# Layer 2 of a fused attention and two-layer MoE kernel in two halves of three slabs over all blocks

## The chip, the core and the metric

The kernel runs on one core of one Trainium2 chip. The metric is the device time of one execution, in microseconds (us). Several executions are timed, and their median is given. A profiled execution gives the trace; its span, from the first to the last instruction, is a little shorter than its own time. Engines: PE is TensorE (matrix products; PEld are its weight loads), DVE is VectorE, ACT is ScalarE, POOL is GpSimd, SP is SyncE, whose queue issues all DMAs here. L12 is line 12 of the kernel.

## The reference

```python
# attention: q, k, v of 4 x 8 heads x 576 positions x 64, a causal window of 64
scores = scale * q @ k.T, outside the window -1e9; softmax; @ v
x = attention, heads joined: 2304 tokens x 512
# layer 1, d_ff 1536
xn = x / sqrt(mean(x * x) + 1e-6) * rms_g
x = (silu(xn @ w_gate) * (xn @ w_val)) @ w_out
# layer 2, d_ff 1536
out = (sigmoid(x @ w_gate2) * (x @ w_val2)) @ w_out2
```

## The kernel before

The 2304 tokens are six blocks of 384. Attention makes a block's 512 x 384 input (st_s, st_tr, st_pv; L387 to L480), beside which its squares are summed and scaled (rms_first: L525 makes diagonal matrices of the scale, the product L526 applies it, L529 takes the result over). Values enter TensorE as pairs of fp16 numbers, high and low, and each product is three matmuls (high x high, high x low, low x high). The split of a block's input is split_first: ScalarE writes the high half (L534), VectorE subtracts it (L535).

Layer 1 treats blocks 0 and 1 plainly: gate and value products (moe_g, moe_v, L574 in mm3, with L587 and L597 on VectorE behind them), the gate's multiplication (moe_h, L608), the output product (moe_o, L623 to L625). The pairs of blocks 2, 3 and 4, 5 of layer 1 and all three pairs of layer 2 use seven products for a 2 x 2 scheme of sub-blocks instead of eight: moe_w(l, p, s) does slab s (256 of d_ff) of pair p, with the products in L784, copies L797 on ScalarE, additions L787 on VectorE and a split into fp16 pairs at the end. The operand of such a product is one of seven *forms* of a pair's input, made by xform_items (split L711, L712) and kept in one set of seven buffers (xform). In layer 2 the forms of pairs 1 and 2 are stored to DRAM (L715) and fetched when the pair's turn comes (fetch_form, L700).

The output products of layer 2 are moe_p(p, ss, c), for the slabs ss and half c of the rows: 7 forms x slabs x 3 matmuls (L888), with PSUM results going to SBUF through a ScalarE copy (L896, the first group of slabs), a scaled addition on VectorE (L898, later groups) or a plain copy (L891). With the last group `give` stores the result (L904).

Weights are 36 packages of 1 MB, 18 a layer (0 to 11: gate and value of six slabs; 12 to 17: output). w_load (L233) fetches one; w_max takes its largest element on VectorE (L243), over the partitions on POOL (L246), and makes scales of it with a few tiny operations (L247 to L254). w_conv and w_split turn it into fp16 pairs (L270 and L335 on ScalarE, L271, L272 and L337 on VectorE); layer 2's packages have sums made for the seven products too (w_sums).

Before the change the weights of layer 2 share one scale over all six slabs (w_l2_scale). It needs every package's maximum, so all 18 are loaded once during layer 1, for w_max alone, and once more for conversion (`again`). The packages' loads and their conversions are hung behind steps of the main sequence (LATER). PLAN2 says for each pair which slabs and which output groups follow:

```python
PLAN2 = [(0, 1, (0, 1), 2, 3, (2, 3), 4, 5, (4, 5)), (0, 1, (0, 1), 2, 3, (2, 3), 4, 5, (4, 5)), (0, 1, 2, (0, 1), 3, 4, (2, 3), 5, (4, 5))]
```

Buffers for intermediate results come from a list of free pieces of the weight areas (`room`, `take`, `early`). The final order of each engine's instructions is fixed by a compressed table (ORDER, applied by arrange after the program is built).

Of the kernel before, what the change touches and what calls it, by code (L numbers as in the profile page):

```python
# [48 lines left out]
AGAIN = (0, 1, 2, 3, 12, 13, 4, 5, 14, 6, 7, 15, 8, 9, 16, 10, 11, 17)  # L49
RAW2 = {j: (2, (56, 64)[i % 2]) for i, j in enumerate(AGAIN)}  # L50
# [61 lines left out]
def fused_kernel(ctx, tc, q, k, v, w_gate, w_val, w_out, rms_g, w2_gate, w2_val, w2_out, const16, const32, out, plan, asked):  # L112
# [47 lines left out]
    ocm = cst.tile([P, 1], F32, name="ocm")  # L160
# [136 lines left out]
    def w_l2_scale():  # L297
        pgv = pw[:, 1, 0:12].rearrange("p (s m) -> p s m", m=2)
        pf = small("pf", NG)
        V.tensor_tensor(out=pf, in0=pgv[:, :, 1], in1=pw[:, 1, 12:18], op=ALU.mult)  # L300
        cm = small("cm")
        V.tensor_reduce(out=cm, in_=pf, axis=AX.X, op=ALU.max)
        ic = small("ic")
        V.reciprocal(out=ic, in_=cm)
        V.tensor_scalar(out=hs2, in0=pf, scalar1=ic, scalar2=2.0 ** -23, op0=ALU.mult, op1=ALU.mult)
        V.tensor_scalar(out=tg2, in0=pgv[:, :, 0], scalar1=pt, scalar2=2.0 ** -39, op0=ALU.mult, op1=ALU.mult)
        V.tensor_scalar(out=ocm, in0=cm, scalar1=pt, scalar2=2.0 ** -28, op0=ALU.mult, op1=ALU.mult)
# [367 lines left out]
    def x1_c(p):  # L675
        px = bx[p]
        be = sp.tile([P, NG], F32, tag="be", name="be", bufs=3)
        V.tensor_scalar(out=be, in0=tg2, scalar1=px, scalar2=None, op0=ALU.mult)
        ga = sp.tile([P, 1], F32, tag="ga", name="ga", bufs=3)
        V.tensor_scalar(out=ga, in0=ocm, scalar1=px, scalar2=None, op0=ALU.mult)  # L680
        bx[p] = (px, be, ga)
# [20 lines left out]
    def xform_items(l, p):  # L702
# [5 lines left out]
        def split(q, x):  # L708
# [80 lines left out]
    def moe_w(l, p, s):  # L789
# [57 lines left out]
        def split(q, x):  # L847
            hf[p, s, q] = hb = early.pop(0) if p == 0 and s < 3 and early else take()
# [24 lines left out]
    hf, acc = {}, {}  # L873
    early = [wl1[:, 63 * KIB + 2 * NMAX * i:63 * KIB + 2 * NMAX * (i + 1)].bitcast(F32) for i in range(6)]
    early += [wl2[:, 28 * KIB + 2 * NMAX * i:28 * KIB + 2 * NMAX * (i + 1)].bitcast(F32) for i in range(8)]
    twice = early[:5]
# [150 lines left out]
    if True:  # L1027
# [60 lines left out]
        lst = sum([pre_max(j) for j in AGAIN], []) + [(("ws2",), w_l2_scale)]  # L1088
# [6 lines left out]
        def again(*js):  # L1095
            return [load(j) for j in js] + interleave(*[conv_rest(1, j) for j in js])
# [6 lines left out]
        for here, x in LATER:  # L1103
            lst = sum([[(("xx", 0, j), lambda j=j: fetch_x(j)) for j in (0, 1)] + xform_items(1, 0) + [(("be",), lambda: x1_c(0))] if y < 0 else again(y) for y in x], [])
# [41 lines left out]
        def step(si, kind, l, b, f):  # L1146
# [205 lines left out]
```

## Time and profile before

| | |
|---|---|
| runs, us | 882.18, 880.96, 880.35; median 880.96 |
| profiled execution, us | 880.94 (span 878.9) |
| busy: PE, DVE, ACT, POOL, us | 847.6, 752.7, 563.2, 35.2 |
| busy PEld, us | 523.8 |
| mean granted TensorE clock | 0.994 of full speed |
| DMA traffic | 103.27 MB in 27433 packets |

An engine's busy time is the time in which at least one of its counted instructions ran. A granted clock of 1.00 is full speed, 2.4 GHz, 0.50 is 1.2 GHz. The first 60 us hold the attention of block 0 and the preparation of layer 1's first weights; layer 1 goes on to somewhat over 400 us, then comes layer 2.

### The profile page before, as it was taken

The numbers are of one execution on the slowest core, as the hardware profiler recorded it, in microseconds if no ns is written. First come the engines' busy times: TensorE is split into PE (matmuls) and PEld (weight loads), VectorE is DVE, ScalarE is ACT, GpSimd is POOL, SyncE is SP. The second block draws the span as 40 slices with busy tenths as digits, with TensorE's granted clock in tenths as the row PEclk, the third lists the DMA queues.
The fourth block names the chain that finished last, engine by engine and source line by source line (L and its number), as shares of the span: only waits on it lengthen the run. The fifth ranks groups of instructions, "written<-read, shape, count | busy, mean of one in ns | idle before, by whom it ended". The sixth has DMA issues, their size and how long they took to land.

```text
span 878.9 us, 15656 instructions
## 1 busy us (share of the span) xinstructions
PE 847.6 (96%) x6084; PEld 523.8 (60%) x6084; DVE 752.7 (86%) x1451; ACT 563.2 (64%) x1226; POOL 35.2 (4%) x42
## 2 busy tenths in 40 slices
PE   4579999999999999999999999999999999999998
PEld 3456666666566666656666655666556665666664
DVE  5999999999998999789999999999865758365677
ACT  5878788677667666457675588767465536255543
POOL 1101100101000210100000000000000000000000
PEclk9989999999999999999999999999999999999999
DMA  9656611223115885322232642305410003200001
GB/s 345 270 202 228 246 38 37 85 66 110 54 54 205 285 306 212 133 72 97 96 132 97 222 156 78 132 4 185 175 45 31 7 1 126 91 1 2 1 1 72
DMA packets 27433, 103.27 MB, mean 117 GB/s; under 512 B 3168, under 2 KB 6624, under 8 KB 20448
## 3 DMA queue, kind: packets, MB, share of 16 engines
q1 hardware_dynamic: 27360, 102.28, 32.8%
q8 instruction: 47, 0.77, 0.4%
q14 instruction: 26, 0.21, 0.1%
HBM read 87.33 MB, written 14.94 MB: 116 GB/s over the span
## 4 chain that ended last, share of the span: by engine, by line
PE 84%; DVE 11%; ACT 2%; DMA 1%; issue 1%; POOL 0%; SPq 0%; ACTq 0%; DVEq 0%
PE bank L784 45%; PE bank L888 14%; PE bank L574 9%; PE bank L623 4%; PE bank L625 4%; PE bank L624 4%; PE bank L404 2%; PE bank L474 2%; PE bank L437 1%; DVE wmax L243 1%; DVE wl L337 1%; DMA wl<-in_moe_w_gate_dram 1%; DVE wl L272 1%; DMA att<-in_q_dram 1%; DVE xhl L718 1%
## 5 line engine op out<-in xcount | busy, mean ns | idle before, releaser
L784 PEld LDWEIGHTS <-wl 128*128 128x128 f16 x2520 | 246.2, 98 | 164.9 <-issue 2.7
L784 PE MATMUL bank<-att,wl 128*128 128x384 f16 x2016 | 339.7, 326 | 0.3 <-DVE xo L787 0.3
L888 PEld LDWEIGHTS <-wl 128*128 128x128 f16 x756 | 73.9, 98 | 49.3 <-issue 0.4
L797 ACT ACTIVATE bank<-bank 128x384 f32<-128x384 f32 x120 | 56.4, 475 | 67.7 <-PE bank L784 40.1
L574 PE MATMUL bank<-xhl,wl 128*128 128x384 f16 x576 | 98.6, 326 | 0.9 <-DVE th L587 0.8
L784 PE MATMUL bank<-xhl,wl 128*128 128x384 f16 x504 | 86.0, 326 | 1.3 <-DVE xhl L712 1.1
L574 PEld LDWEIGHTS <-wl 128*128 128x128 f16 x576 | 55.7, 98 | 38.0 <-issue 2.5
L888 PE MATMUL bank<-xhl,wl 128*128 128x384 f16 x354 | 68.7, 326 | 0.0
L335 ACT ACTIVATE wl<-wl,isc 128x1024 f16<-128x1024 f32 (+1 forms) x48 | 53.8, 1148 | 17.9 <-DVE wl L314 6.6
L623 PE MATMUL bank<-wl,wl 128*128 128x384 f16 x192 | 62.7, 327 | 0.0
L624 PE MATMUL bank<-wl,wl 128*128 128x384 f16 x192 | 62.6, 326 | 0.0
L625 PE MATMUL bank<-wl,wl 128*128 128x384 f16 x192 | 62.6, 326 | 0.0
L427 ACT ACTIVATE sm<-sm,su 128x128 f32<-128x128 f32 x120 | 38.3, 392 | 15.7 <-DVE su L422 12.2
L270 ACT ACTIVATE wl<-wl 128x1024 f32<-128x1024 f32 x36 | 41.5, 1155 | 6.9 <-DMA wl<-in_moe_w_out_dram 4.3
L243 DVE TENSOR_REDUCE wmax<-wl 128x1 f32<-128x1024 f32 x36 | 43.5, 1209 | 0.6 <-DMA wl<-in_moe_w_gate_dram 0.6
L420 ACT ACTIVATE sm<-sm,nm 128x128 f32<-128x128 f32 x96 | 37.2, 390 | 9.0 <-DVE nm L414 8.9
L787 DVE TENSOR_TENSOR xhl<-xhl,bank 128x384 f32<-128x384 f32 x49 | 26.6, 549 | 15.8 <-PE bank L784 14.9
L623 PEld LDWEIGHTS <-wl 128*128 128x128 f16 x288 | 28.2, 98 | 18.9 <-issue 1.5
L625 PEld LDWEIGHTS <-wl 128*128 128x128 f16 x288 | 28.2, 98 | 18.6
L337 DVE SCALAR_TENSOR_TENSOR wl<-wl,isc,wl 128x1024 f16<-128x1024 f32 (+1 forms) x32 | 38.0, 1193 | 1.2 <-ACT wl L335 1.2
L624 PEld LDWEIGHTS <-wl 128*128 128x128 f16 x288 | 28.2, 98 | 17.1
L829 DVE SCALAR_TENSOR_TENSOR xhl<-xhl,bank 128x384 f32<-128x384 f32 x32 | 17.6, 549 | 19.6 <-PE bank L784 12.9
(399 smaller groups left out, 1489.5 us busy)
## 6 DMA issues: line engine op xcount, KB each, us to landing
wl<-in_moe_w_val_dram SPq DMA_DIRECT2D x18, 1024.0 KB, 4.9
wl<-in_moe_w_gate_dram SPq DMA_DIRECT2D x18, 1024.0 KB, 5.2
wl<-in_moe_w_out_dram SPq DMA_DIRECT2D x18, 1024.0 KB, 5.2
vn<-in_v_dram SPq DMA_DIRECT2D x27, 256.0 KB, 4.0
f<-xhl SPq DMA_DIRECT2D x14, 384.0 KB, 3.1
att<-f SPq DMA_DIRECT2D x14, 384.0 KB, 3.8
att<-in_k_dram SPq DMA_DIRECT2D x13, 384.0 KB, 5.3
att<-in_q_dram SPq DMA_DIRECT2D x17, 256.0 KB, 5.1
```

The lines of the kernel that those rows point to most:

```text
L243: V.tensor_reduce(out=r1[:, i:i + 1], in_=wraw(layer, j + i)[:, :, 1].bitcast(F32), axis=AX.X, op=ALU.max, apply_absolute_value=True)
L270: A.activation(out=y.bitcast(F32), in_=hi.bitcast(F32), func=AF.Prelu, scale=2.0 ** -112, alpha=-2.0 ** 32)
L335: A.activation(out=hi, in_=y, func=AF.Copy, scale=sc)
L337: V.scalar_tensor_tensor(out=lo, in0=y, scalar=sc, in1=hi, op0=ALU.mult, op1=ALU.subtract)
L427: A.activation(out=s[e][:, c], in_=s[e][:, c], func=AF.Copy, scale=su[:, j:j + 1])
L574: T.matmul(pb[:, 0:n], lhsT=w_, rhs=x_, start=(c == 0), stop=(c == m - 1))
L623: T.matmul(o[c][:, 0:n], lhsT=wh[:, cs], rhs=hi, start=st, stop=False)
L624: T.matmul(o[c][:, 0:n], lhsT=wh[:, cs], rhs=lo, start=False, stop=False)
L625: T.matmul(o[c][:, 0:n], lhsT=wl[:, cs], rhs=hi, start=False, stop=en)
L784: T.matmul(pb[:, 0:NMAX], lhsT=w_, rhs=x[:, t, kk], start=first and kk == n == 0, stop=kk == 1 and n == 2, skip_group_check=not first)
L797: A.activation(out=o[:, 0:NMAX], in_=i[:, 0:NMAX], func=AF.Copy)
L888: T.matmul(pb[:, 0:NMAX], lhsT=w_, rhs=x[:, t], start=st and s == ss[0] and n == 0, stop=s == ss[-1] and n == 2, skip_group_check=not st)
```

## The change

Layer 2 is done in two halves of three slabs each, (0, 1, 2) and (3, 4, 5), and each half goes over all three pairs before the other begins, in the order of the new PLAN2 (W12 is slab 2 of pair 1, P20 the output group of pair 2 and half 0). Each half has its own scale (w_l2_scale(h), x1_c(p, h)), so that the scales of the second half need no maxima until late. Five packages (FIRST) are still loaded early for their maximum alone and loaded again; the other 13 are loaded, have their maximum taken and are converted in one go, late. The output sums run over three slabs. For pairs 0 and 1 the sums of the first half are stored to DRAM (parked, 16 stores) and fetched back before the second half's group (16 fetches). As TensorE comes back to pairs 0 and 1, the forms of pair 0 are stored too, and the seven forms are fetched four times instead of twice. The lists of free buffers are arranged anew, and the whole ORDER table is new. DMAs of SP: 54 weight loads become 41, 14 form fetches 28, 14 form stores 21.

```diff
-PLAN2 = [(0, 1, (0, 1), 2, 3, (2, 3), 4, 5, (4, 5)), (0, 1, (0, 1), 2, 3, (2, 3), 4, 5, (4, 5)), (0, 1, 2, (0, 1), 3, 4, (2, 3), 5, (4, 5))]
+PLAN2 = "W00 W01 W02 W10 P00 W11 W12 W20 P10 W21 W22 W23 P20 W24 W25 W03 P21 W04 W05 W13 W14 W15 P01 P11"
...
-AGAIN = (0, 1, 2, 3, 12, 13, 4, 5, 14, 6, 7, 15, 8, 9, 16, 10, 11, 17)
+FIRST = (4, 5, 12, 13, 14)
...
-    ocm = cst.tile([P, 1], F32, name="ocm")
+    ocm = cst.tile([P, 2], F32, name="ocm")
...
-    def w_l2_scale():
-        pgv = pw[:, 1, 0:12].rearrange("p (s m) -> p s m", m=2)
-        pf = small("pf", NG)
-        V.tensor_tensor(out=pf, in0=pgv[:, :, 1], in1=pw[:, 1, 12:18], op=ALU.mult)
+    def w_l2_scale(h):
+        js = slice(3 * h, 3 * h + 3)
+        pgv = pw[:, 1, 6 * h:6 * h + 6].rearrange("p (s m) -> p s m", m=2)
+        pf = small("pf", 3)
+        V.tensor_tensor(out=pf, in0=pgv[:, :, 1], in1=pw[:, 1, 12 + 3 * h:15 + 3 * h], op=ALU.mult)
...
-            if l and p:
+            if l:
                 spill[p, 'f', q] = dp.tile([P, 2, 2, NMAX], F16, name=f"f{p}{q}")
                 SY.dma_start(out=spill[p, 'f', q], in_=t)
...
     def moe_p(p, ss, c):
-        sc = bx[p][2]
         first, last = ss[0] == 0, ss[-1] == NG - 1
+        sc = bx[p][2][:, 0:1] if first else bx[p][2][:, 1:2]
+        for k in ((0, 0), (1, 0), (1, 1), (0, 1)):
+            if last and p < 2:
+                acc[p, c, k] = take()
+                SY.dma_start(out=acc[p, c, k], in_=parked[p, c, k])
...
                 SY.dma_start(out=out[r0:r0 + P, t0:t0 + NMAX], in_=y)
                 room.append(y)
+            elif p < 2:
+                y = acc.pop((p, c, k))
+                parked[p, c, k] = dp.tile([P, NMAX], F32, name=f"f{7 + p}{c}{k[0]}{k[1]}")
+                SY.dma_start(out=parked[p, c, k], in_=y)
+                room.append(y)
...
-        lst = sum([pre_max(j) for j in AGAIN], []) + [(("ws2",), w_l2_scale)]
+        lst = sum([pre_max(j) for j in FIRST], [])
         place(lst, pos["W", 0, 1, 3] + 1, pos["W", 0, 2, 0], post)
...
-        def again(*js):
-            return [load(j) for j in js] + interleave(*[conv_rest(1, j) for j in js])
+        def later(x):
...
+            if x == "s0":
+                return [(("ws2",), lambda: w_l2_scale(0))]
+            if x == "s1":
+                return [(("ws2", 1), lambda: w_l2_scale(1))] + [(("be", p), lambda p=p: x1_c(p, 1)) for p in (2, 0, 1)]
+            j = int(x.lstrip("r"))
+            return [load(j)] + ([] if x[0] == "r" else [(("m", 1, j), lambda: w_max(1, j))]) + conv_rest(1, j)
...
-            a, e = [(("W", 1, 0, 0), ("W", 1, 0, 2)), (("W", 1, 1, 1), ("W", 1, 1, 4))][p - 1]
-            place(lst, pos[a] + 1, pos[e], mid)
-            place([(("xg", p, q), lambda p=p, q=q: fetch_form(p, q)) for q in (0, 6, 5, 1, 4, 3, 2)], pos["W", 1, p - 1, 5] + 1, pos["W", 1, p - 1, 5] + 2, mid)
+            place(lst, pos["W", 1, p - 1, 0] + 1, pos["W", 1, p - 1, 2], mid)
+        for p, x in ((1, ("W", 1, 0, 2)), (2, ("W", 1, 1, 2)), (0, ("W", 1, 2, 5)), (1, ("W", 1, 0, 5))):
+            place([(("xg", p, q), lambda p=p, q=q: fetch_form(p, q)) for q in (0, 6, 5, 1, 4, 3, 2)], pos[x] + 1, pos[x] + 2, mid)
...
 ORDER = (
-    'c-n1O349aP*3Z2&*(TehN%yAvN(-f>g|<MgECobBcq)hjJ_V5qZt!@1`X1o+DT06?A|NP;f`UIpKvq!%w8#$Kcj!)=J!zKC%zcw4O=g0fG?}?M_uT(k|'
+    'c-n1O2|yFq*3P*zNk~XY0s%x;1=$gd;6@cHNKr(gF4byLtCqUdKGZ6;E?BW{eJ)h1QlATIUFvVEh+^FZQB)KZL}U|C7BP?j0STG8e?TBJ(HUkk%)R&Av'
...
```

The order on the engines differs in most places. Three of them follow, row by row, with line, operation, output<-inputs by the names of buffers, and the shape of the output. Line numbers of the changed kernel are one or two higher in the attention and the weights (L243 is L244 there, L272 is L273, L337 is L339, L525 is L527, L535 is L537), and a few lower or higher in layer 2 (L700 is L698, L904 is L909).

The first is VectorE where block 0's scale goes into the diagonal matrices (xhl_266 is the buffer of these matrices, wl_76 and wl_75 the areas of layer 2's and layer 1's weights). Before:

```order
L454 SCALAR_TENSOR_TENSOR ry_305<-rh_307,ry_305 128x2
L254 TENSOR_SCALAR tg_86<-pw,pgam 128x1
L453 TENSOR_TENSOR rh_369<-rh_369,ra_366 128x1
L525 TENSOR_SCALAR xhl_266<-ident,ry_305 128x128
L454 SCALAR_TENSOR_TENSOR ry_367<-rh_369,ry_367 128x1
L525 TENSOR_SCALAR xhl_266<-ident,ry_305 128x128
L525 TENSOR_SCALAR xhl_266<-ident,ry_367 128x128
L272 SCALAR_TENSOR_TENSOR wl_76<-wl_75,wl_76 128x1024
```

and changed:

```order
L456 SCALAR_TENSOR_TENSOR ry_305<-rh_307,ry_305 128x2
L454 SCALAR_TENSOR_TENSOR rh_369<-ry_367 128x1
L527 TENSOR_SCALAR xhl_266<-ident,ry_305 128x128
L455 TENSOR_TENSOR rh_369<-rh_369,ra_366 128x1
L423 TENSOR_SCALAR su_184<-su_184 128x8
L456 SCALAR_TENSOR_TENSOR ry_367<-rh_369,ry_367 128x1
L527 TENSOR_SCALAR xhl_266<-ident,ry_305 128x128
L424 RECIPROCAL su_184<-su_184 128x8
L527 TENSOR_SCALAR xhl_266<-ident,ry_367 128x128
L244 TENSOR_REDUCE wmax_492<-wl_76 128x1
```

The conversion L272 no longer stands between the diagonal matrices and L529, and a max pass (L244) stands behind them that was ahead.

The second is VectorE at the split of block 0's input (xhl_327 is the split's buffer, th_474 a buffer behind the gate product). Before:

```order
L529 SCALAR_TENSOR_TENSOR wl_76<-wl_76,cg,bank_206 128x256
L337 SCALAR_TENSOR_TENSOR wl_75<-wl_76,isc,wl_75 128x1024
L535 TENSOR_TENSOR xhl_327<-wl_76,xhl_327 128x4x128
L535 TENSOR_TENSOR xhl_327<-wl_76,xhl_327 128x4x256
L248 TENSOR_SCALAR pw<-amax 128x2
L272 SCALAR_TENSOR_TENSOR wl_76<-wl_75,wl_76 128x1024
L252 TENSOR_SCALAR isc<-pw 128x2
L411 TENSOR_REDUCE nm_145<-bank_163 128x4
L271 TENSOR_SCALAR wl_76<-wl_76 128x1024
L337 SCALAR_TENSOR_TENSOR wl_75<-wl_76,isc,wl_75 128x1024
```

and changed:

```order
L531 SCALAR_TENSOR_TENSOR wl_76<-wl_76,cg,bank_206 128x256
L244 TENSOR_REDUCE wmax_492<-wl_76 128x1
L537 TENSOR_TENSOR xhl_327<-wl_76,xhl_327 128x4x128
L537 TENSOR_TENSOR xhl_327<-wl_76,xhl_327 128x4x256
L413 TENSOR_REDUCE nm_145<-bank_164 128x4
L255 TENSOR_SCALAR tg_86<-pw,pgam 128x1
L413 TENSOR_REDUCE nm_145<-bank_163 128x4
L272 TENSOR_SCALAR wl_76<-wl_76 128x1024
L418 TENSOR_SCALAR nm_145<-nm_145 128x8
L273 SCALAR_TENSOR_TENSOR wl_76<-wl_75,wl_76 128x1024
L589 SCALAR_TENSOR_TENSOR th_474<-th_474,bank_200 128x384
L339 SCALAR_TENSOR_TENSOR wl_75<-wl_76,isc,wl_75 128x1024
```

A conversion L337 stands directly ahead of the split before, a max pass in the changed order, and the conversions that came ahead of the split or soon behind it come later.

The third is SP's queue at a change of pair in layer 2 (att holds the forms, f_... are their copies in DRAM, xhl_1288 is the buffer in which new ones are made). Before, from pair 1 to pair 2:

```order
L715 DMA f_6801<-xhl_1288 128x1536
L700 DMA att<-f_6797 128x1536
L715 DMA f_6926<-xhl_1288 128x1536
L700 DMA att<-f_6560 128x1536
L700 DMA att<-f_6926 128x1536
L700 DMA att<-f_6789 128x1536
L700 DMA att<-f_6793 128x1536
L700 DMA att<-f_6801 128x1536
L904 DMA out_dram<-xhl_147 128x384
```

and changed, from pair 2 back to pair 0, where the copies were stored at the end of layer 1 and in layer 2's first steps:

```order
L234 DMA wl_76<-in_moe_w_out_dram 128x2048
L698 DMA att<-f_4798 128x1536
L698 DMA att<-f_4779 128x1536
L698 DMA att<-f_4790 128x1536
L698 DMA att<-f_4802 128x1536
L698 DMA att<-f_4785 128x1536
L698 DMA att<-f_4794 128x1536
L698 DMA att<-f_4807 128x1536
L909 DMA out_dram<-xhl_327 128x384
L909 DMA out_dram<-wl_75 128x384
L698 DMA att<-f_5212 128x1536
```

Before, stores of forms and fetches alternate; in the changed order the seven fetches follow one another.

## Rows read from the trace of the kernel before

**Rows 1.** The page, part 1: busy time, share of the span, instructions.
```profile
PE 847.6 (96%) x6084; PEld 523.8 (60%) x6084; DVE 752.7 (86%) x1451; ACT 563.2 (64%) x1226; POOL 35.2 (4%) x42
```

**Rows 2.** Stretches: from:to, length, busy of PE, PEld, DVE, ACT, POOL; PEclk, DMA share, GB/s.
```profile
7.30:20.00 12.70, 5.59 (x69) 4.04 (x69) 10.60 (x23) 7.83 (x34) 2.21 (x2) 1.00 1.01 406
20.00:42.20 22.20, 13.17 (x174) 11.09 (x175) 21.60 (x40) 19.74 (x47) 3.25 (x2) 1.00 0.69 268
42.20:52.50 10.30, 5.18 (x30) 3.82 (x31) 9.70 (x41) 7.58 (x21) 0.92 (x1) 0.50 0.43 167
60.00:120.00 60.00, 59.46 (x528) 38.81 (x527) 58.66 (x129) 46.58 (x118) 6.53 (x8) 1.00 0.61 224
400.00:640.00 240.00, 239.98 (x1476) 144.19 (x1475) 232.97 (x434) 164.65 (x270) 1.65 (x1) 1.00 0.36 126
640.00:860.00 220.00, 220.00 (x1354) 132.33 (x1353) 139.44 (x262) 112.31 (x224) 0.00 (x0) 1.00 0.09 31
```

**Rows 3.** Waits of TensorE: engine line <- what it waited for: us, times, longest.
```profile
PE bank L437 <- DVE wl L429: 5.8, 2, 5.0
PE bank L404 <- DMA wl<-in_q_dram: 4.4, 1, 4.4
PE bank L526 <- DVE xhl L525: 4.3, 1, 4.3
...
PE bank L784 <- DVE xhl L712: 1.1, 1, 1.1
PE bank L574 <- DVE th L587: 0.8, 2, 0.6
...
PE bank L784 <- DVE xo L787: 0.5, 2, 0.3
```

**Rows 4.** Groups of VectorE's instructions, 0 to 53 us: busy us, mean ns, idle before.
```profile
L243 DVE TENSOR_REDUCE wmax<-wl 128x1 f32<-128x1024 f32 x8 | 9.7, 1210 | 0.6 <-DMA wl<-in_moe_w_gate_dram 0.6
L272 DVE SCALAR_TENSOR_TENSOR wl<-wl,wl 128x1024 int32<-128x1024 int32 x6 | 7.2, 1221 | 0.1
L337 DVE SCALAR_TENSOR_TENSOR wl<-wl,isc,wl 128x1024 f16<-128x1024 f32 x5 | 6.4, 1273 | 0.0
...
L271 DVE TENSOR_SCALAR wl<-wl 128x1024 int32<-128x1024 int32 x7 | 4.8, 691 | 0.0
```

**Rows 5.** Timeline at the first gate product: start us, us, engine, line, operation.
```profile
47.41 0.47 DVE L525 TENSOR_SCALAR xhl<-ident,ry 128x128 f32<-128x128 f32 x2
...
47.48 1.68 PE L526 MATMUL bank<-xhl,wl 128*128 128x128 f32 x6 [4.29 <-DVE xhl L525]
...
52.74 1.82 DVE L535 TENSOR_TENSOR xhl<-wl,xhl 128x512 f16<-128x512 f32 x2
...
54.21 2.35 PE L574 MATMUL bank<-xhl,wl 128*128 128x384 f16 x12
...
55.69 0.16 DVE L252 TENSOR_SCALAR isc<-pw 128x2 int32<-128x2 int32 x1
55.76 0.68 DVE L411 TENSOR_REDUCE nm<-bank 128x4 f32<-128x512 f32 x1
...
56.35 0.68 DVE L271 TENSOR_SCALAR wl<-wl 128x1024 int32<-128x1024 int32 x1
```

**Rows 6.** Lines L535 and L608 on VectorE: ns min/median/max, first and last start.
```profile
L535 DVE TENSOR_TENSOR xhl<-att,xhl x1: 1759/1759/1759, 115.0 to 115.0; 128x1536 f16<-128x1536 f32 x1
...
L608 DVE TENSOR_TENSOR wl<-th,wl x24: 543/550/571, 65.4 to 222.6; 128x384 f16<-128x384 f32 x24
```

**Rows 7.** Line L898 on VectorE, the commonest form.
```profile
L898 DVE SCALAR_TENSOR_TENSOR wl<-bank,ga,wl x30: 606/610/618, 707.8 to 875.5; 128x384 f32<-128x384 f32 x30
```

**Rows 8.** Line L700 on SP's queue: ns of an issue, and landing.
```profile
L700 SPq DMA_DIRECT2D att<-f x14: 319/424/1291, 606.4 to 756.6; - x14
...
DMA to landing us min/median/max: 3.0/3.8/6.9
```

**Rows 9.** Timeline of the end.
```profile
875.48 0.62 DVE L898 SCALAR_TENSOR_TENSOR wl<-bank,ga,wl 128x384 f32<-128x384 f32 x1 [0.36 <-PE bank L888]
```

More of the change, by code (lines that the diff above doesn't have):

```diff
@@ L673, in x1_scale, with x1_c @@
         sxs[p] = sx
[L675 to L681, printed above, removed]
+    def x1_c(p, h=0):
+        if not h:
+            bx[p] = (bx[p], sp.tile([P, NG], F32, tag="be", name="be", bufs=3), sp.tile([P, 2], F32, tag="ga", name="ga", bufs=3))
+        px, be, ga = bx[p]
+        js = slice(3 * h, 3 * h + 3)
+        V.tensor_scalar(out=be[:, js], in0=tg2[:, js], scalar1=px, scalar2=None, op0=ALU.mult)
+        V.tensor_scalar(out=ga[:, h:h + 1], in0=ocm[:, h:h + 1], scalar1=px, scalar2=None, op0=ALU.mult)
     forms = []
@@ L847, in split @@
         def split(q, x):
-            hf[p, s, q] = hb = early.pop(0) if p == 0 and s < 3 and early else take()
+            hf[p, s, q] = hb = early.pop(0) if p < 2 and s < 3 and early else take()
             h = hb.bitcast(F16).rearrange("p (t n) -> p t n", t=2)
@@ L871, in moe_w, with cut @@
         room.append(b21)
[L873 to L876, printed above, removed]
+    hf, acc, parked = {}, {}, {}
+    def cut(home, lo, hi):
+        return [home[:, i:i + 2 * NMAX].bitcast(F32) for i in range(lo * KIB, hi * KIB - 2 * NMAX + 1, 2 * NMAX)]
+    once = cut(wl2, 7, 28) + cut(wl1, 56, 63)
+    twice = cut(wl1, 63, 72) + cut(wl2, 28, 42)
+    early = once + twice
     def moe_p(p, ss, c):
-        sc = bx[p][2]
         first, last = ss[0] == 0, ss[-1] == NG - 1
+        sc = bx[p][2][:, 0:1] if first else bx[p][2][:, 1:2]
[3 more added lines that the diff above has]
+                SY.dma_start(out=acc[p, c, k], in_=parked[p, c, k])
         def go(pb, a, b, st=False):
@@ L937, in moe_p @@
                     hb = hf.pop((p, s, q))
-                    if p == 0 and s < 2:
-                        early.extend([hb] if any(hb is x for x in twice) else [])
-                    elif p or s > 2 or not any(hb is x for x in twice):
+                    if any(hb is x for x in twice) and p == 0:
+                        early.append(hb)
+                    elif not any(hb is x for x in once + twice):
                         room.append(hb)
@@ L996, in fused_kernel @@
         oo(0, 2 * p + 1, range(FC))
-    for p in range(NB // 2):
-        for x in PLAN2[p]:
-            main.append(("W", 1, p, x) if isinstance(x, int) else ("P", 1, p, x))
+    halves = ((0, 1, 2), (3, 4, 5))
+    for x in PLAN2.split():
+        p, i = int(x[1]), int(x[2])
+        main.append(("W", 1, p, i) if x[0] == "W" else ("P", 1, p, halves[i]))
     pos = {x: i for i, x in enumerate(main)}
@@ L1103, in fused_kernel @@
         for here, x in LATER:
-            lst = sum([[(("xx", 0, j), lambda j=j: fetch_x(j)) for j in (0, 1)] + xform_items(1, 0) + [(("be",), lambda: x1_c(0))] if y < 0 else again(y) for y in x], [])
+            lst = sum(map(later, x.split()), [])
             place(lst, pos[here] + 1, pos[here] + 2, mid)
@@ L1152, in step @@
                     moe_p(b, f, c)
+                if (b, f) == (2, (0, 1, 2)):
+                    for home, lo in ((wl2, 49), (wl1, 21), (wl1, 35)):
+                        room.extend(cut(home, lo, lo + 7))
                 return
@@ L1245 @@
+    'H{7_4B1UA<`~<<;e6P)7{H0aqKu4WBvkLlm`%mTNN&IkqlWE$DB0M=PC3RJMwFO3bC`(3MsNeAGXu)%{5VG43-dC>6@T1^%<l$ZaWRKQxR~7rVpj2B_N'
+    'N5%+XNf4vq4deS=KNqxNBpY^C3+35>Ds4CZpya3{0y3YU_D!!JH4eapRVb)swT4f|)3o^N}X4n__A7AqI36ItKRV3TC(IEY9t`gQ28*mvpsQ-Arxt{nt'
+    'I|{{c<gxS{'
 )
```

132 lines of the change are left out of this document (61 added, 71 removed).

## The prediction

> **What bounds the kernel now.** I read the page's engine shares first: TensorE is busy 96% of a span of 878.9 us, VectorE 86% [rows 1]. A mean over the span hides stages, so the table of stretches comes next [rows 2]. From 60 us on TensorE has next to no holes: it is busy 59.46 of 60, 239.98 of 240 and 220.00 of 220 us. Its pace there is that of its own matmuls: 1476 in 240 us are 162.6 ns each, 1354 in 220 us are 162.5 ns, although VectorE falls from 232.97 busy of 240 to 139.44 of 220. 384 columns in 160 ns would be one for each cycle of the granted 2.4 GHz (PEclk 1.00). So after 60 us only fewer matmuls or fewer waits can shorten the run, and the change leaves every matmul in place, 5478 in both programs.
>
> The holes are in the first 60 us. The waits of TensorE [rows 3] name VectorE and a load: 5.8 us on the softmax scaling (L429), 4.4 on q, 4.3 on L525. In those stretches VectorE is busy 21.60 of 22.20 and 9.70 of 10.30 us [rows 2]: it runs on while TensorE starves. Beside the attention of block 0 it prepares layer 1's first weights there: 8 max passes L243, 7 L271, 6 L272, 5 L337 [rows 4]. The way into layer 1 stands in the timeline [rows 5]. At 47.48 TensorE is let go by L525, then it runs nearly without a gap, at half clock until 52.5, through the products that VectorE feeds on (L526, L529) and the attention's next ones, to the first gate product L574 at 54.21, with the second split subtraction L535 (52.74 to 54.56) beside it. From there TensorE is full. **How much VectorE has done before L525 and before L535 decides when L574 starts**, and all that follows is shifted by that.
>
> **The change, part by part.**
>
> *Ahead of L525 and L535 of block 0 (place A).* TensorE's order is the same in both programs up to L574. Ahead of the first L525 VectorE has two L243, one L271 and five operations of a few elements less. Ahead of L535 it has one L271, one L272, one L337 and two of the small ones less; nothing new stands ahead of either. Neighbours on VectorE overlap by 0.085 us or so: L411 is 0.68 long and the next starts 0.59 later, the small L252 is 0.16 long and the next starts 0.07 later [rows 5]. The price of one is its mean [rows 4] less that: L243 1.125, L272 1.14, L337 1.19, L271 0.60, a small one 0.07. L525: 2.25 + 0.60 + 0.35 = 3.2 us earlier. L535: 0.60 + 1.14 + 1.19 + 0.14 = 3.07. Taken: **-3.1 us**, as long as the inputs are there in time.
>
> *Clock.* From 42.2 to 52.5 us the granted clock was 0.50, that is 1.2 GHz, after a stretch in which TensorE was busy 13.17 of 22.20 us [rows 2]. It was full again 5.0 us after TensorE began to run on at 47.48. If it comes back as long after the earlier start, this costs nothing. If it stays down until 52.5 whatever happens, the 3.2 us won are run at half pace, and 1.6 of them are lost. **+0.8 us**, the middle, with 0 and 1.6 as bounds.
>
> *Ahead of the split of block 1 (place B).* In before this L535 starts at 115.0. Ahead of it stand 14 max passes instead of 17, two L247 and one L608 (550 ns) less [rows 6]: 3 x 1.125 + 0.12 + 0.47 = 4.0 us less work. From 60 to 120 us VectorE was 58.66 of 60 busy while TensorE hardly waited [rows 2], so the two ran level; now VectorE is 0.9 us further ahead of a TensorE that starts 3.1 earlier, and the start is not given back. The 0.8 us of L574 behind L587 [rows 3] may go too; left out.
>
> *Max passes of layer 2.* All 18 weights of layer 2 were loaded during layer 1 for their largest elements alone, now five. 13 x 1.125 = 14.6 us of VectorE and 13 loads of 1 MB leave layer 1, and the passes come back in layer 2. Of TensorE's waits past 60 us, 1.1 us on L712 and 0.5 on L787 are VectorE's [rows 3]; with that lead I take both as gone: **-1.6 us**. In layer 2 the passes lie beside TensorE's work: conversions now run on into the stretch where VectorE was 63% busy (139.44 of 220) [rows 2]. Without that cover, in the stretch where it is 97% busy, they would cost up to 14.6 us.
>
> *Sums of three slabs.* 36 fewer L898 of 610 ns [rows 7], 22 us of VectorE, and 12 fewer copies L891 on ScalarE. TensorE waits for neither in layer 2: 0, but this pays for the passes that came there.
>
> *Parked sums.* 16 stores and 16 fetches of 192 KB. A fetch stands ahead of its product group; the nearest row is a form's fetch, 3.0 to 6.9 us to landing [rows 8], and a group is 63 products, 10 us. The DMA share from 640 us on is 0.09 [rows 2]. 0, with one late landing as the bound, 2 us.
>
> *Form switches.* The seven forms of one pair lie in one set of buffers. From one pair to another each is fetched after its last reader: twice in before (14 fetches), now four times (28). Counted in the orders, between the product that lets SP issue a fetch and the first that reads it there were 90 to 168 products, 14.6 to 27 us; now 33 to 99, 5.4 to 16 us, the two shortest 33 and 36, and 14 of 28 between 42 and 54 (6.8 to 8.8). Landing takes 3.0, in the median 3.8, at most 6.9 us, after an issue of 0.42 [rows 8]. The median fits every gap; the longest seen misses three, by 1.9, 1.4 and 0.5 us. Taken **0**, bound +3.8. The Trainium skill, DMA: Bandwidth & Descriptors, section "Anatomy of one DMA — SWDGE (gpsimd) path", speaks against the change here: a DMA has a fixed cost of about 2.0 us however small, and a wait on a semaphore is made on the issuing sequencer, before dispatch. By it every added fetch pays 2 us after its release; the 3.0 us measured hold them already, so the sum by the rule is the same unless a gap falls under that.
>
> *The end* stays: the last L898 at 875.48 [rows 9], then a store.
>
> Sum: -3.1 + 0.8 - 1.6 = -3.9. The profiled execution took 880.94 us, 2.04 more than its span and 0.02 under the median of the three runs. 880.94 - 3.9 = **877.0**.
>
> **Rivals.**
>
> *The head start is used up.* The DMA share is 1.01 from 7.3 to 20 us and 0.69 behind [rows 2], and 4.4 us of waiting is a load's [rows 3]. If the loads and not VectorE's work pace block 0, L525 comes when it came. For it: those loads stay, in nearly the same order. Against: VectorE idles only 0.60 us in the 22.20 behind. What is left is part of the later waits, 0.5 to 1.6: about 880, no change. Chance 0.17.
>
> *Slower: the form fetches miss their gaps.* Seven of 384 KB go out in a burst beside stores and weights. At 406 GB/s, the rate where the share is 1.01 [rows 2], seven take 6.8 us; the last, behind all the others, would land 3.0 + 6.8 = 9.8 us after the first release, against gaps of 5.4 to 7.8. That is 2 to 4.4 us at each of four switches; at 2 us each 877 + 8 = **885**. It decides from 1.4 us a switch, where four of them eat the gain of 3.9 and 1.8 more. Against: TensorE reads the seven one after another, the share is 0.36 from 400 to 640 us, and in before no wait of L784 on such a fetch is listed [rows 3]. Chance 0.07.
>
> *Much faster: VectorE held layer 2.* Over the whole program VectorE has 36 x 0.525 - 0.4 = 18.5 us less to do; had TensorE been paced by that unseen, 881 - 18.5 = 862. The Trainium skill, Perfetto Trace Analysis, section "Identifying the Most-Contended Engine", holds that matmul busy time tells little of how close TensorE is to its limit, and asks for the share of weight loads. That share is 60% [rows 1], which would leave room. Against: 162.5 ns with VectorE 97% and 63% busy alike [rows 2]. Chance 0.03.
>
> **How the numbers follow.** The forecast has 0.73. Its best end has no cost of the clock, and L574's wait of 0.8 and place B's 0.9 besides: 877.0 - 0.8 - 0.8 - 0.9 = 874.5. The other end is the first rival with its smallest gain, 880.5. Left out are the last two rivals, 0.10, and as much of the tails. A measurement of this kernel tells about 0.2%, 1.8 us, from no change. Faster 0.73 + 0.03 = 0.76; same 0.17; slower 0.07.
>
> **What would show it.** Right: L574 begins at 51 to 52.5 us and TensorE is full from there; the waits on L712 and L787 are gone; no wait of L784 on a form's fetch; matmuls at 162 to 163 ns in layer 2; 41 weight loads. Wrong: L574 at 54 as before, with waits on loads in the first 50 us; L784 waiting for att at the switches W02 to W10, W12 to W20, W25 to W03, W05 to W13; L888 waiting for a parked sum; a stretch of layer 2 with VectorE full and TensorE not.

## The result, and the profile after

The changed kernel took 873.38 us in the median of 4 runs (872.16 to 874.75), the kernel before 880.79: a ratio of 0.9914, 95% interval 0.9895 to 0.9932. It was timed twice more beside the experiments, 5 runs each: 875.16 us (0.9942, 0.9928 to 0.9956) and 875.47 us (0.9943, 0.9931 to 0.9956). So the gain is 4.8 to 7.4 us where I forecast 3.9; the first median lies 1.1 us under my range, the two later ones inside it. The profiled run took 874.75 us, 6.2 less than that of before, with a span of 872.6 us; this is what the lines can explain.

The page's first part, to be read against [rows 1]:

```profile
PE 846.4 (97%) x6084; PEld 523.7 (60%) x6084; DVE 736.5 (84%) x1427; ACT 555.1 (64%) x1214; POOL 31.3 (4%) x42
```

VectorE lost 16.2 us of work and TensorE next to none. The waits of TensorE, answering to [rows 3]:

```profile
PE bank L528 <- DVE xhl L527: 2.5, 1, 2.5
...
PE bank L782 <- DVE xo L785: 0.6, 2, 0.3
PE bank L576 <- DVE th L589: 0.4, 1, 0.4
PE bank L782 <- DVE att L710: 0.3, 1, 0.3
PE bank L782 <- DMA att<-f: 0.2, 1, 0.2
```

L785, L589 and L710 are L787, L587 and L712 of before. The wait for the scale matrices is 2.5 us where it was 4.3. The 1.1 us on the forms' split, at 229 us before, has gone, but 0.3 us on the split for the next pair has come, at 373 us. The waits on L785 are 0.6 us where they were 0.5, and the switches of forms cost 0.2 us. Stretches, as in [rows 2]:

```profile
45.00:50.00 5.00, 4.83 (x45) 3.61 (x44) 4.92 (x12) 4.96 (x11) 0.55 (x1) 0.50 0.63 252
50.00:55.00 5.00, 5.00 (x64) 3.29 (x57) 5.00 (x9) 4.56 (x8) 0.18 (x1) 1.00 0.20 56
...
400.00:640.00 240.00, 239.75 (x1476) 144.15 (x1475) 218.88 (x408) 155.54 (x262) 4.81 (x9) 1.00 0.42 144
640.00:860.00 220.00, 220.00 (x1356) 132.46 (x1355) 160.49 (x314) 118.24 (x226) 2.59 (x4) 1.00 0.24 79
```

The clock is full again from 50 us, 2.5 us sooner than before. From 400 us on TensorE does the same 1476 matmuls in 240 us, while VectorE has gone from 232.97 to 218.88 us there and up to 160.49 behind. The start, as in [rows 5]:

```profile
44.08 1.65 PE L528 MATMUL bank<-xhl,wl 128*128 128x128 f32 x6 [2.49 <-DVE xhl L527]
...
51.23 8.95 PE L576 MATMUL bank<-xhl,wl 128*128 128x384 f16 x54
```

Where the time went is best read by setting equal products beside each other. The table has the start of the n-th matmul of a line, counted in each trace, in us. The lines are those of before (L574 gate and value products, L784 those of the seven-product scheme, L888 layer 2's output); 289 is the first of block 1, the 421st L784 lies in layer 1's first pair, the 1156th in layer 2's first slabs, which both plans begin with. The rows under the second are repeats of the changed kernel (a_again, a_third) and the experiments below.

| kernel | L574 1st | L574 25th | L574 289th | L784 421st | L784 1156th | last L888 |
|---|---|---|---|---|---|---|
| before | 54.21 | 59.34 | 116.89 | 325.83 | 530.18 | 875.12 |
| changed | 51.23 | 55.15 | 111.40 | 319.51 | 523.80 | 868.75 |
| a_again | 51.26 | 55.17 | 111.43 | 319.92 | 524.21 | 869.62 |
| a_third | 51.74 | 55.65 | 111.90 | 320.13 | 524.42 | 870.03 |
| b_head51 | 50.09 | 58.09 | 117.01 | 325.92 | 530.06 | 874.95 |
| b_head130 | 50.22 | 54.13 | 110.41 | 325.22 | 529.59 | 874.51 |
| b_head280 | 50.28 | 54.19 | 110.44 | 342.07 | 546.46 | 891.60 |
| a_head270 | 52.94 | 58.12 | 115.67 | 323.85 | 528.13 | 873.34 |
| a_head54 | 53.88 | 57.80 | 114.06 | 322.54 | 526.83 | 871.59 |
| a_head130 | 53.14 | 57.95 | 115.52 | 323.43 | 527.72 | 872.93 |
| b_short | 52.53 | 57.53 | 115.31 | 324.15 | 528.52 | 873.47 |
| a_start | 49.49 | 57.26 | 113.52 | 321.60 | 525.88 | 871.11 |
| b_order_m1 | 51.78 | 55.69 | 111.95 | 321.42 | 545.35 | 890.28 |
| b_m2 | 50.64 | 54.55 | 110.81 | 320.41 | 529.79 | 874.73 |
| b_m4 | 49.19 | 53.10 | 109.36 | 318.45 | 535.49 | 885.92 |
| a_long | 50.29 | 54.20 | 110.45 | 318.53 | 535.06 | 879.59 |

The changed kernel is 2.98 us ahead at the first gate product, 5.5 at block 1's, 6.3 in layer 1's first pair, and then 6.4 in layer 2 and at the end. **All of the gain is there by 320 us; layer 2 itself, which the change rewrites, runs neither faster nor slower.**

The first column must be read with care. Up to the first gate product before, b_short, a_head54, a_head130 and a_head270 have one and the same order, and it begins at 52.53 to 54.21 us; eleven profiles with the changed kernel's order there (all other rows but a_start, and b_m3 below at 49.90) have it at 49.19 to 51.78 us. The means, 53.3 and 50.6, differ by 2.7 us, a single pair by 0.8 to 5.0. The distance from there to the 289th product repeats much better: 62.68 us in before and 62.78 in b_short, 60.17, 60.17 and 60.16 in the three profiles of the changed kernel.

### The profile page after: what moved, and what is told of

The parts are those of the page before. It is cut to its first block, busy times and chain, and to the rows that moved or that the text cites. A ratio compares the mean times of both kernels' runs of the same rounds, so it can differ in the third digit from the quotient of the medians.

```text
span 872.6 us, 15623 instructions
## 1 busy us (share of the span) xinstructions
PE 846.4 (97%) x6084; PEld 523.7 (60%) x6084; DVE 736.5 (84%) x1427; ACT 555.1 (64%) x1214; POOL 31.3 (4%) x42
## 4 chain that ended last, share of the span: by engine, by line
PE 88%; DVE 8%; DMA 2%; ACT 1%; issue 0%; POOL 0%; SPq 0%; DVEq 0%; ACTq 0%; POOLq 0%
PE bank L782 45%; PE bank L893 14%; PE bank L576 10%; PE bank L625 4%; PE bank L626 4%; PE bank L627 4%; PE bank L406 2%; PE bank L476 2%; PE bank L439 1%; DMA att<-f 1%; DVE wmax L244 1%; DMA att<-in_q_dram 1%; DMA wl<-in_moe_w_gate_dram 1%; DVE wl L339 1%; DVE wl L273 1%
## 5 line engine op out<-in xcount | busy, mean ns | idle before, releaser
L782 PEld LDWEIGHTS <-wl 128*128 128x128 f16 x2520 | 246.0, 98 | 164.9 <-issue 2.1
L782 PE MATMUL bank<-att,wl 128*128 128x384 f16 x2016 | 338.1, 326 | 0.6 <-DVE att L710 0.3
L795 ACT ACTIVATE bank<-bank 128x384 f32<-128x384 f32 x120 | 56.9, 478 | 75.4 <-PE bank L782 31.3
L576 PE MATMUL bank<-xhl,wl 128*128 128x384 f16 x576 | 97.6, 326 | 0.4 <-DVE th L589 0.4
L782 PE MATMUL bank<-xhl,wl 128*128 128x384 f16 x504 | 86.2, 326 | 0.6 <-DVE xo L785 0.6
L576 PEld LDWEIGHTS <-wl 128*128 128x128 f16 x576 | 55.5, 98 | 36.9 <-issue 1.3
L337 ACT ACTIVATE wl<-wl,isc 128x1024 f16<-128x1024 f32 (+1 forms) x48 | 54.2, 1142 | 9.6 <-DVE wl L317 6.3
L893 PE MATMUL bank<-xhl,wl 128*128 128x384 f16 x264 | 51.6, 326 | 0.0
L244 DVE TENSOR_REDUCE wmax<-wl 128x1 f32<-128x1024 f32 x36 | 43.6, 1213 | 4.8 <-DMA wl<-in_moe_w_out_dram 2.5
L893 PE MATMUL bank<-wl 128*128 128x384 f16 x222 | 45.9, 326 | 0.0
L339 DVE SCALAR_TENSOR_TENSOR wl<-wl,isc,wl 128x1024 f16<-128x1024 f32 (+1 forms) x32 | 38.1, 1196 | 1.1 <-ACT wl L337 0.9
L273 DVE SCALAR_TENSOR_TENSOR wl<-wl,wl 128x1024 int32<-128x1024 int32 x28 | 34.3, 1225 | 0.3
```

The lines of the kernel that those rows point to most:

```text
L244: V.tensor_reduce(out=r1[:, i:i + 1], in_=wraw(layer, j + i)[:, :, 1].bitcast(F32), axis=AX.X, op=ALU.max, apply_absolute_value=True)
L273: V.scalar_tensor_tensor(out=y if (layer, j) in PACKED else hi, in0=y, scalar=3, in1=lo, op0=ALU.logical_shift_left, op1=ALU.bitwise_or)
L337: A.activation(out=hi, in_=y, func=AF.Copy, scale=sc)
L339: V.scalar_tensor_tensor(out=lo, in0=y, scalar=sc, in1=hi, op0=ALU.mult, op1=ALU.subtract)
L576: T.matmul(pb[:, 0:n], lhsT=w_, rhs=x_, start=(c == 0), stop=(c == m - 1))
L782: T.matmul(pb[:, 0:NMAX], lhsT=w_, rhs=x[:, t, kk], start=first and kk == n == 0, stop=kk == 1 and n == 2, skip_group_check=not first)
```

## The experiments

**Is it the order of layer 1?** Both programs begin with the same 1457 operations, up to the first load for layer 2, so the order of these can be exchanged. HEAD holds how many of them each engine had started by 280, 130 or 51.2 us in the changed kernel (b_...: put into the kernel before), or by 270, 130 or 54.2 us in the kernel before (a_...: put into the changed one); ORDER2 is the other kernel's table.

```diff
+    seq2 = [k for k in seq2 if k < 1457]
+    of = lambda s, e: [k for k in s if ops[k][0] == e]
+    head = {e: of(seq2, e)[:HEAD.get(e, 0)] for e in ENGINES}
+    seq = sum([head[e] + [k for k in of(seq, e) if k not in head[e]] for e in ENGINES], [])
```

> The changed kernel with the first part of each engine's order (to 270 us) as it was before; the two halves of layer 2 and all that comes with them kept. Theory 1: 880.5 us, like before, since layer 2's new plan is worth nothing by itself. Theory 2: 876 to 877.5 us, the start lost and the rest kept.

a_head270 took 879.87 us, 0.9998 of before (0.9989 to 1.0007): the new layer 2 with the old order of layer 1 gains nothing. Two shorter heads say how much each stretch holds, beside the changed kernel at 875.47 us in the same comparison:

> The changed kernel with the first part of each engine's order as before, up to the first gate product alone (what before started until 54.2 us). My first term: L576 begins 3 us later and this stays to the end: 877.5 us. If the conversions done early in return give VectorE a lead behind, and TensorE's waits there fall: 875 us.

> The same up to 130 us. By the lead that the changed kernel has at that place, 5.5 us: 879 to 880 us. If the second stretch of layer 1 gives some back: 877 us.

> The changed kernel as it is, beside the others: 873.4 to 875.2 us, as measured twice.

a_head54 took 877.80 us, a_head130 879.34. Undoing the start costs 2.3 us, the stretch up to 130 us 1.5 more, and by a_head270 what lies behind about 0.5, no more than the noise. My first term was 3.1. In the table a_head54, with the changed order behind the start, takes 60.18 us from the first gate product to block 1's, like the changed kernel; a_head130 and a_head270 take 62.38 and 62.73, like before.

**Does an earlier start keep?** In the kernel before it does not:

> The kernel before with the changed kernel's order up to the first gate product alone (what starts before 51.2 us). My prediction's first term: L574 begins 3 us earlier. If the start is kept to the end and the waits behind it stay: 878 us. If the earlier start also takes the later waits away, by the lead that VectorE then has: 874.5 to 876 us. If VectorE, level with TensorE behind it, takes it back: 880 us.

b_head51 took 881.74 us (1.0018, 1.0009 to 1.0027). The waits of TensorE name where the start went:

```profile
PE bank L574 <- DVE th L587: 3.7, 1, 3.7
```

By the table it is 4.1 us ahead at the first gate product, 1.3 at the 25th and 0.1 behind at the 289th: the conversions moved behind the split are paid at the next place that needs VectorE. They are paid with more than the wait. It ends at 58.09 us, and then the granted clock was 0.50, that is 1.2 GHz, for 3.4 us, in which TensorE was busy throughout:

```profile
58.60:62.00 3.40, 3.40 (x12) 1.60 (x11) 2.43 (x4) 2.17 (x6) 0.00 (x0) 0.50 0.81 320
```

At half clock half of that, 1.7 us by estimate, is lost as well. From the first gate product to the 289th it takes 66.92 us, 4.2 more than before.

> The same up to 130 us, the end of block 1's first products. Theory 1: the lead at 120 us was 5.5 us, so 875.5 us, with the wait of 1.3 us at the first L784 of 227 us as in before if nothing later is changed. If only the start counts: 878 us.

b_head130 took 880.24 us: 6.5 us ahead at the 289th product, 0.6 at the 421st of L784. Again the lead goes at the place where the orders meet, first in a wait, on ScalarE's L439, which ends at 133.43 us, and then in the clock:

```profile
PE bank L474 <- ACT sm L439: 2.8, 2, 2.5
```
```profile
133.20:140.00 6.80, 6.49 (x71) 4.61 (x72) 6.46 (x9) 5.21 (x7) 0.00 (x0) 0.50 0.24 82
```

The wait of 2.5 us and, by the same estimate, half of the 6.49 us that TensorE was busy at half clock make 5.7 of the 5.9 us lost.

> The kernel before, with the first part of each engine's order (what the changed kernel starts before 280 us, layer 1 up to its second pair; the operations are the same in both programs there) taken from the changed kernel; all of layer 2 as before. Theory 1 (the whole gain comes from the order of the first 280 us): about 874.5 us, 6.3 less than before, and the first gate product at 51.2 us. Theory 2 (the gain past the start comes from what left layer 1, 13 max passes and 13 loads, or from layer 2's halves): 878 us, the start's 3 us alone.

b_head280 took 895.82 us. It is 7 us ahead up to 276 us, then TensorE stands still. First TensorE's wait, then VectorE's timeline there:

```profile
PE bank L624 <- DVE xo L840: 18.4, 1, 18.4
```
```profile
294.34 1.22 DVE L243 TENSOR_REDUCE wmax<-wl 128x1 f32<-128x1024 f32 x1 [4.90 <-DMA wl<-in_moe_w_gate_dram]
```

From 277 to 290 us VectorE makes up slab sums (L312 to L315, L753 to L763) that the new order leaves for later; they read the area that layer 2's early loads overwrite, so these come late, and the max passes, for which VectorE waits 4.9 us on a load, stand ahead of L840. That gave the second theory: the new order defers work into the stretch from which the change takes 13 max passes and loads. Below, theory A is that the order of layer 1 is all, theory B that the room which these passes and loads leave is needed too. I tried one more step of deferring on the changed kernel (rows of VectorE, one conversion and one max pass moved):

```diff
-L339 SCALAR_TENSOR_TENSOR wl_75<-wl_76,isc,wl_75 128x1024
 L453 SCALAR_TENSOR_TENSOR ry_367<-rh_369,ry_367 128x1
...
-L244 TENSOR_REDUCE wmax_492<-wl_76 128x1
+L339 SCALAR_TENSOR_TENSOR wl_75<-wl_76,isc,wl_75 128x1024
...
 L537 TENSOR_TENSOR xhl_327<-wl_76,xhl_327 128x4x256
+L244 TENSOR_REDUCE wmax_492<-wl_76 128x1
```

> The changed kernel with one more conversion (L339) moved behind the diagonal matrices (L527) and one max pass (L244) moved behind the split of block 0 (L537). If VectorE's work ahead of L527 decides the start: L576 begins 1 us earlier, 872.4 us. If the moved work is only paid behind it, as the order up to 51 us alone showed on the kernel before: 873.4 us, with a wait of L576 on L589 of about 1 us.

> The changed kernel as it is, beside the others on the same chip: 873.4 us, as measured first.

a_start took 877.74 us against 875.16 for the changed kernel: slower, and slower than either expectation. L576 begins at 49.49 us, which lies within the spread of the changed order, and then stops for the second half of the split, which now comes behind other work:

```profile
PE bank L576 <- DVE xhl L537: 2.0, 1, 2.0
```

From 52.7 to 56.1 us the granted clock was 0.50. The way to block 1's first product takes 64.03 us where it took 60.17.

**Is it the 13 passes?** First alone, in the old order:

```diff
-                V.tensor_reduce(out=r1[:, i:i + 1], in_=wraw(layer, j + i)[:, :, 1].bitcast(F32), axis=AX.X, op=ALU.max, apply_absolute_value=True)
+                V.tensor_reduce(out=r1[:, i:i + 1], in_=wraw(layer, j + i)[:, 0:8 if layer == 1 and j not in (4, 5, 12, 13, 14) else 1024, 1].bitcast(F32), axis=AX.X, op=ALU.max, apply_absolute_value=True)
```

> The kernel before with the 13 early max passes of layer 2 that the change moves away cut to 8 of 1024 columns each, all else and the order as before (the scales and so the output then rest on part of the weights). My prediction's third term has VectorE's relief in layer 1 take the waits on L712 and L787 away: 1.6 us, 879. Theory A and B both: these passes run from 264 us on, behind those waits, so nothing: 880.3 us.

b_short took 879.89 us (0.9994, 0.9985 to 1.0003). The passes' time alone is worth nothing; their loads stayed. Then under the new order of layer 1, in the kernel before (b_order_m1: only ORDER differs; b_m2: that order, with the passes cut as above and `w_load(1, j, 16)` for these 13 early loads):

> The kernel before, all of layer 2 as it was (18 max passes early, all packages loaded twice, pairs one after another), with the changed kernel's order in the 1457 operations that both programs begin with (layer 1 up to the first load for layer 2), and the 18 early loads and max passes moved back as far as these operations push them, some 25 to 55 us later, to about 320 to 379 us. Theory A (the order of layer 1 is all): 874.5 us, and layer 2's halves are not needed for it. Theory B (the new order of layer 1 defers slab sums and so needs the room that 13 max passes and loads leave from 264 to 353 us): the passes now stand in the way, and TensorE waits some 5 to 18 us between 300 and 380 us: 880 to 892 us.

> The kernel before with the changed kernel's order of layer 1, as in the run at 896.9 us, but the 13 early loads and max passes that the change moves away cut to 8 of 1024 columns each, where they stand (the scales and so the output then rest on part of these weights); five stay whole. Theory B (these 13 stand in the way of the new order of layer 1, and their leaving is what pays for it): the 18 us of waits between 280 and 400 us go, and the gain of layer 1 stays: 873 to 877 us. If my order of the operations behind them is what stalls, and not the passes: 885 us or more.

b_order_m1 took 896.90 us, b_m2 880.57. Cutting 13 passes and loads takes 16.3 us off in the new order, where cutting the passes alone took 0.4 off in the old. But b_m2 does not keep its lead: 5.4 us at the 421st L784, 0.4 at the 1156th. It goes between 335 and 393 us, where VectorE is busy 30.67 of 40 us up to 360 and 35.90 of the next 40. So the passes are not all of it, or my order behind the common part is poor. Two more orders of mine with the old layer 2 entire:

> The kernel before, layer 2 and all its work as it was, with the changed kernel's order of layer 1 as in the run at 896.9 us, and the operations behind it put in a new order in which an engine takes what is ready, the 18 early max passes and their loads last, some 45 us later than before; nothing is cut. Theory A (the gain is the order of layer 1, and layer 2's halves are not needed for it): 873 to 876 us. Theory B (the 13 passes and loads stand in the way wherever they are put): 880 us or more, with TensorE waiting on VectorE between 300 and 420 us.

> The kernel before, layer 2 and all its work as it was, with the changed kernel's order in the operations that both begin with, and the operations behind them ordered once more, this time with room for the transfers: a consumer stands behind its load by what loads that share the queues took in the traces. Nothing is cut. Theory A (the gain is the order of layer 1, and the old layer 2 can follow it): 873 to 877 us. Theory B (13 passes and 13 loads more, beside the slab sums that the new order defers to the same stretch, cost what it gains): 879 us or more, with the lead of 6 us there at 280 us and gone by 500.

b_m3 took 907.89 us, b_m4 894.25. Stretches of b_m4:

```profile
320.00:360.00 40.00, 37.64 (x306) 23.02 (x305) 35.78 (x79) 26.47 (x76) 4.38 (x11) 1.00 0.76 270
360.00:400.00 40.00, 37.20 (x218) 21.60 (x217) 38.52 (x80) 15.81 (x29) 8.27 (x10) 0.96 0.81 295
400.00:440.00 40.00, 38.84 (x235) 22.75 (x234) 39.42 (x79) 28.78 (x45) 0.00 (x0) 1.00 0.30 107
```

It is 7.4 us ahead at 320 us and 3.8 behind at 409. Most is lost ahead of 400 us, where VectorE is not full: TensorE waits there 2.5 us on the forms' split (L712) and 1.8 on a copy of ScalarE (L797), VectorE itself 2.4 us on a load, and the DMA share is 0.76 and 0.81. From 400 us on VectorE is full and TensorE is not, which costs 1.2 us of these 40. Before, VectorE was 39.69 us busy of the 40 from 400 us on, with TensorE full, so a thing deferred to here has no place. In the changed kernel it is 32.31 there. So b_m4 shows a want of room for the smaller part of its loss; the larger part can as well come of the loads or of my order. The last run puts the work back into the changed kernel under its own order:

```diff
+                x, o = wraw(layer, j + i)[:, :, 1].bitcast(F32), r1[:, i:i + 1]
+                if layer == 1 and j in FIRST:
+                    x, o = x.unsqueeze(1).to_broadcast([P, 4, 1024]), r1
+                V.tensor_reduce(out=o, in_=x, axis=AX.X, op=ALU.max, apply_absolute_value=True)
```

> The changed kernel with its five early max passes (323 to 352 us) each made four times as long, by reading the package four times over: some 16 us of VectorE's work more in that stretch, as much as the 13 passes that the change moved away, with no load and no other order. Theory B (the new order needs the room that those passes left): TensorE waits after 323 us, 4 to 16 us, 879 to 891 us. Theory A (VectorE has room there anyway): 873.4 to 875.5 us as before.

a_long took 885.64 us. It is 7.3 us ahead of before at the 421st L784 and 4.9 behind at the 1156th. The stretch where it happens, first a_long, then the changed kernel:

```profile
320.00:360.00 40.00, 34.08 (x250) 20.30 (x250) 34.90 (x44) 20.84 (x60) 1.77 (x3) 0.91 0.37 135
```
```profile
320.00:360.00 40.00, 39.94 (x326) 25.32 (x325) 28.80 (x56) 25.72 (x70) 5.21 (x6) 1.00 0.51 188
```

Some 16 us of VectorE's work in that place cost 10.2 us against the second repeat, as theory B expected. But VectorE is not full there: it is busy 34.90 of 40 us, and 33.30 of the next 40. The passes come in blocks of 4.4 us. TensorE's longest wait begins while VectorE is in the second block and ends 2 us behind it, and then TensorE runs at half clock for 4.5 us (lines are three higher here: L785 is the changed kernel's L782, L798 its L795):

```profile
PE bank L785 <- ACT bank L798: 4.7, 1, 4.7
```
```profile
332.10:339.00 6.90, 4.50 (x15) 2.08 (x15) 3.29 (x7) 0.94 (x2) 1.19 (x2) 0.51 0.57 209
```

So the run shows that long blocks of VectorE's work cannot stand in that place. Whether the same work in small pieces would cost as much was not tried, and that no order of the old layer 2 could do without the room is not shown.

**Can order give more?** Both kernels in orders of mine, nothing else changed:

> The changed kernel, every operation as it is, in a new order on all engines in which an engine takes what is ready by the durations of its trace. Theory A's other side: TensorE is idle some 21 us ahead of the first gate product in the changed kernel too, and if order is what decides, a part of it can be had, 6 to 12 us: 863 to 869 us. If the loads at a share of 1.0 in the first 20 us set the start: 872 to 875 us.

> The same for the kernel before, with all its 18 early loads and max passes and its old plan of layer 2. Theory A: below the changed kernel, 866 to 872 us, without any of the change. Theory B: 877 us or more.

> The changed kernel, every operation as it is, ordered anew in small steps on all engines but TensorE's own first stretch, with that room for transfers. If order still decides in the changed kernel, a lead of 2 us at the first gate product that grows to 5 us by 300 us and 8 to 10 us by the end: 864 to 869 us. If TensorE is at its pace and the rest is loads: 873 to 876 us.

a_free took 931.94 us, b_free 937.82, a_opt 881.46. None is of use. In a_free the first gate product comes at 57.88 us; TensorE waits 15.1 us for one load (the constants, L400), where that wait is 2.8 us in the changed kernel. I had put consumers right behind loads that share the queues, and an engine that runs in order stands with all its work behind such a load. No version beat the changed kernel.

## Why the prediction was right and where it was wrong

The direction, the bound and layer 2 were right. TensorE's pace in layer 2 is unchanged (1476 matmuls in 240 us), the parked sums appear in no wait, and the form switches cost 0.2 us, 0.7 and 0.9 in the repeats, although a landing took up to 8.6 us in the changed kernel, over the 6.9 that I took as the longest. The rival of missed gaps did not come about; nor did the one in which VectorE held layer 2: from 400 to 640 us it had 14 us less to do, from 640 to 860 us 21 us more, and the pace stayed as it was. The rival of the used-up start, by which the scale matrices come when they came, did not either. The weight loads' share, which by the Trainium skill (Perfetto Trace Analysis, section "Identifying the Most-Contended Engine") is to be used, with the share of peak work, in place of matmul busy time to tell how near TensorE is to its limit, is 60% before and after and showed none of this; the holes between matmuls did.

**The start, -3.1**, was sized right: TensorE is let go by the scale matrices 3.40 us earlier (47.48 and 44.08), the first gate product begins 2.98 earlier, and a_head54 has 2.3 in run time. That one pair of profiles comes so near is in part luck, with a spread of 1.7 us and more for the same order; the means differ by 2.7. **The clock, +0.8**, came out at about 0.4: the clock was back at 50.0 us, 2.5 us sooner where TensorE was let go 3.4 us sooner, and from there to the first gate product it takes 7.15 us instead of 6.73. Both together are 0.7 us of the error, the next term is 1.8.

**The later waits, -1.6, was the step that failed, in size and in reason.** Behind the first gate product the lead grows by 3.4 us, from 2.98 to 6.37, and 2.5 of them are there by block 1's first product, a stretch for which I had taken nothing. From the first gate product to 325 us both programs run the same 2296 matmul records; summing what their starts lie further apart than the median of their line, where that is over 0.12 us, gives 10.69 us before and 7.37 after: 3.3 us gone. The waits of the list in that stretch sum to 3.2 us and 0.9. The two that I had counted, 1.1 and 0.5, gave 0.7 together: the first left 0.3 us at the next pair, the second stayed. The rest is 0.8 on L574, which I left out and of which 0.4 are left, and two on ScalarE, in the transposes and the value products of the attention, which I did not show and which are gone:

```profile
PE bank L437 <- ACT sm L427: 0.8, 2, 0.5
...
PE bank L474 <- ACT sm L439: 0.3, 1, 0.3
```

The reason was wrong too. I had the 13 max passes relieve VectorE ahead of these waits. In the kernel before, the early passes of layer 2 begin at 277 us. The wait on L712 lies at 229, ahead of them; those on L787 lie at 304 and 384, and stay when the passes are cut (b_short). With the passes gone and the old order up to 270 us nothing is gained (a_head270). What takes the waits away is the order of layer 1: with it the way to block 1's first product is 2.5 us shorter, whatever the start (a_head54), and without it it is not. Counted in the traces, VectorE has begun 3.0 us less work by the first gate product, 4.9 less by the 25th and 3.9 less by the 289th (three max passes fewer). The heads exchange the order of every engine, so that VectorE's share decides is read from this count and from the waits, and was not tried apart.

Why the changed kernel keeps this lead stays open in part. The new order lost it with the old layer 2 in every run (b_head280, b_order_m1, b_m2, b_m3, b_m4), and 13 passes and loads less took 16.3 us off there; so their leaving counts. But with them cut b_m2 still lost its lead, in a stretch where VectorE was not full, and a_long put the work back in long blocks alone. Whether a better order could have done it in the old layer 2 is not known: all that were tried are mine.

My sentence that the start "is not given back" rested on VectorE and TensorE running level from 60 to 120 us. In that state it is given back, as b_head51 shows; it keeps here because the order behind it was changed as well. **Place B** was said to put VectorE 4.0 us of work, and 0.9 us net, further ahead; the work is right (3.9), but by block 1's first product the lead was 2.5 more.

## What to carry to other kernels

In an engine that runs in order and without gaps, moving work behind a critical point helped here only where the order behind it had changed too: look first for the stretch that is to take the work, and ask what the change takes out of it. A wait of TensorE in a full stretch cost more than its length here, as the granted clock fell to 0.50 behind it: 2.5 us became 5.7 in b_head130, 2.0 became 3.9 in a_start. Compare two traces by the start of equal products; the point at which the lead stops growing tells which part of a change paid, and that can be a part that the diff hardly mentions. Sum all waits of the critical engine in the stretches that a change reorders, whichever engine they name, and not those for which you have a story.

## What was not expected of the hardware

In the repeat of the changed kernel at 875.16 us the granted clock was 0.81 and 0.67 in the first two stretches of 20 us, where the first profile had 1.00 and 0.99, and yet the first gate product came at 51.26 us against 51.23:

```profile
0.00:20.00 20.00, 9.31 (x106) 6.07 (x106) 11.93 (x26) 10.13 (x40) 1.72 (x6) 0.81 0.90 346
20.00:40.00 20.00, 14.63 (x174) 12.30 (x175) 18.39 (x42) 17.29 (x42) 1.10 (x2) 0.67 0.65 237
```

There TensorE waits for loads and VectorE, and the halved clock cost nothing that shows. Where TensorE had work at once, as behind the waits of b_head51 and b_head130, it did cost. A landing of a form of 384 KB took 2.9 to 8.6 us in one profile and up to 9.2 in another, with the median at 3.8 in both.
